# Reordering the start of a fused attention and feed-forward kernel: batch 0's front, and where batch 3 is loaded, cast and reduced

## The chip, the cores and the metric

The kernel runs on one core of one Trainium2 chip. The metric is device time in microseconds (us) for one execution, lower is better. Before the change the median of four runs is 284.23 us (284.03 to 284.37).

A core has five engines, each with its own instruction queue, worked in order: TensorE (PE; its weight loads are listed as PEld), VectorE (DVE), ScalarE (ACT), GpSimd (POOL) and SyncE (SP), which here only issues DMAs. Engines wait for each other by semaphores.

## The reference

q, k and v have shape (8 batches, 8 heads, 576 rows, 64 columns). The attention is the linear kind: softmax of q over its columns, softmax of k over its rows, a 64x64 product per head, and q times that product. Its result x (4608 x 512) goes through a two-layer feed-forward block with an exact GELU.

```python
q_s = np.exp(q - np.max(q, axis=-1, keepdims=True));  q_s /= np.sum(q_s, axis=-1, keepdims=True) + 1e-09
k_s = np.exp(k - np.max(k, axis=2, keepdims=True));   k_s /= np.sum(k_s, axis=2, keepdims=True) + 1e-09
kv  = np.einsum('bhsd,bhse->bhde', k_s, v)
x   = np.einsum('bhsd,bhde->bhse', q_s, kv)          # then (B*S, H*D)
h   = x @ w_in                                       # 512 -> 2048
out = (0.5 * h * (1.0 + erf(h / sqrt(2)))) @ w_out   # 2048 -> 512
```

## The kernel before, in words

The order of instructions is written out by hand (`tc.manual_schedule()`): each engine does its work in the order in which the program lists it, and a helper called early in the listing stands early in every queue that it uses, SP's among them.

The program works by chunks. Chunks 0 to 7 are batches 0 to 7, with the first 512 of the 576 rows each; chunk 8 holds the last 64 rows of all batches. For each batch there is a front and two phases.

The front of batch b:

- `load(b)`: three DMAs from SP, q, k and v, into buffers that exist twice (`f32in`, `bufs=2`), so that batch b + 2 reuses those of batch b. Batches 0 and 1 are loaded in parts.
- `exp_q`, `exp_k`: exponentials on ACT. `table(...)` is a tiny activation that makes ACT load the table of a function ahead of its use.
- `norm_q`: the row sums of exp(q) and their reciprocals on DVE, then the multiplication, on POOL unless DVE is named. `norm_q(b, 0, 2)` and `norm_q(b, 1, 2, nc.vector)` do the two halves of the heads, the first on POOL and the second on DVE.
- The transposed q (`qT`): for batches 0 and 1 by TensorE (`tp_mm`: eight transposes per half; `tp_evac`: the copy from PSUM, DVE by default; `tp_step` is both), later by a transposing DMA on SP (`xbar_step`).
- `cast_v`: v to bf16, one of four head pairs at a time, on DVE unless another engine is named; `cast_v_all` is all four on DVE.
- `kv_mm`: the product of exp(k) and v for two head pairs, 36 small matmuls; a column of ones in v gives the softmax sums of k along with it. `kv_norm` divides by them on DVE. `kv_step` is both halves and one division. The buffers for exp(k) and for v exist twice, by b modulo 2.
- `x_mm`, `x_evac`: q times kv, and its copy to SBUF as `xT` on DVE, or on ACT with "s". `x_all` is the whole.

Then `h_phase(c)`: 64 matmuls of `xT` with w_in, 16 tiles of four, and a GELU on ACT for each tile. `y_phase(c)`: four output tiles j of 16 matmuls each, accumulated in one of two PSUM buffers (`psum_y`, `bufs=2`); `y_out` copies each on DVE into one of four buffers and stores it from SP. Because DVE works in order, j = 2 can start only when DVE has reached and done the copy of j = 0. Chunk 0's y phase is written out separately and interleaved with batch 1's front (lines 464 to 511).

Both phases take a dictionary of insertions. In `h_phase` the key is the tile after whose GELU the insertion is listed; in `y_phase` it is (j, t), after matmul t of tile j. The front of a later batch is put into the phases of an earlier chunk in this way:

- lines 425 to 454, batch 0's front. `warm(n)` issues n matmuls on zeros into a scratch buffer.
- lines 464 to 511, chunk 0's y phase and batch 1's front.
- line 512, chunk 1's h phase with `cast_v_all(2)`; line 513, `load(3)`.
- lines 516 to 527, the exponentials of batches 2 and 3, and chunk 1's y phase with the rest of batch 2's front.
- lines 531 to 536, `front3`: the rest of batch 3's front, and `load(4)`; it is listed after the first GELU of chunk 2's h phase.
- lines 538 to 564: chunks 2 to 8, each with the front of the batch two further on.

At the beginning SP is given the loads of batch 0, of both weight matrices, and of batches 1 and 2, one after the other (lines 413 to 422). `cast_wi` and `cast_wo` convert the weights, the first two tiles of w_in on POOL.

Of the kernel before, what the change touches and what calls it, by code (L numbers as in the profile page):

```python
# [10 lines left out]
AF = mybir.ActivationFunctionType  # L11
# [5 lines left out]
def kernel(  # L17
# [16 lines left out]
    nc = tc.nc  # L34
# [6 lines left out]
    HP = H // 2  # L41
# [30 lines left out]
    def setup_tiles():  # L72
        nc.vector.memset(scr, 0.0)  # L73
        for i in range(2):
            nc.vector.memset(v_aug[i][:, :, :, D:D + 1], 1.0)

    def table(func):
        nc.scalar.activation(out=scr[:, 1:2], in_=scr[:, 0:1], func=func)  # L78
# [3 lines left out]
    def load_main(b, name, t, parts=1):  # L82
        f = f32in.tile([128, 2048], FP32, tag=name + "f")
        f = f.rearrange("p (h f) -> p h f", h=H)
        st[b][name + "f"] = f
        src = t[b, :, 0:M, :].rearrange("h (p j) d -> p h (j d)", j=J)
        n = H // parts
        for i in range(parts):
            nc.sync.dma_start(out=f[:, i * n:(i + 1) * n, :], in_=src[:, i * n:(i + 1) * n, :])
# [9 lines left out]
    def load(b):  # L99
        load_main(b, "q", q)  # L100
        load_pair(b, "k", k)
        load_pair(b, "v", v)
# [11 lines left out]
    def exp_q(b, parts=1):  # L114

        e = attn_sb.tile([128, J, H, D], BF16, tag="eq")
        st[b]["eq"] = e
        dst = e.rearrange("p j h d -> p h j d")
        src = st[b]["qf"]
        if b == B:  # L120
            src = src.rearrange("p j h d -> p h j d")
        else:
            src = src.rearrange("p h (j d) -> p h j d", j=J)
        if parts == 1:
            sets = [(slice(i, None, 4), slice(u, None, 4)) for i, u in ((0, 0), (1, 1), (2, 3), (3, 2))]
        else:
            sets = []
            for h in (0, 4):
                sets += [(slice(h + i, h + i + n), slice(h + u, h + u + n))
                         for i, u, n in ((0, 0, 2), (2, 3, 1), (3, 2, 1))]  # L130
        for i, u in sets:
            nc.scalar.activation(out=dst[:, i], in_=src[:, u], func=AF.Exp)  # L132

    def exp_k(b, parts=1):
        n = HP // parts
        for i in range(0, HP, n):
            nc.scalar.activation(  # L137
                out=ek[b % 2][:, i:i + n],
                in_=st[b]["kf"][:, i:i + n].rearrange("p x (n d) -> p x n d", n=NS),
                func=AF.Exp,  # L140
            )

    def cast_v(b, hp, eng=nc.vector):
        eng.tensor_copy(  # L144
            out=v_aug[b % 2][:, hp, :, 0:D],
            in_=st[b]["vf"][:, hp, :].rearrange("p (n d) -> p n d", n=NS),
        )

    def cast_v_all(b):
        for hp in range(HP):  # L150
            cast_v(b, hp)
# [18 lines left out]
    def kv_norm(b, h0, h1):  # L170

        ps = st[b]["kv"]
        m = h1 - h0
        rec = small.tile([128, 2, 2], FP32, tag="reck")
        nc.vector.reciprocal(rec[:, :, 0:m], ps[:, :, h0:h1, D])
        nc.vector.tensor_tensor(  # L176
            out=kvc[b].rearrange("p (h i) d -> p i h d", i=2)[:, :, h0:h1],
            in0=ps[:, :, h0:h1, 0:D],
            in1=rec[:, :, 0:m].unsqueeze(3).to_broadcast([128, 2, m, D]), op=ALU.mult,
        )  # L180

    def kv_step(b):
        kv_mm(b, 0)
        kv_mm(b, 1)
        kv_norm(b, 0, 2)
# [16 lines left out]
    def tp_mm(b, half):  # L202
        if half == 0:
            st[b]["qT"] = attn_sb.tile([128, J, HP, 128], BF16, tag="qT", name="qT")
        pool, tag = (psum_h, "h") if half == 1 else (psum_a, "a")
        ps = pool.tile([128, J, 2, 128], BF16, tag=tag)
        st[b][f"tp{half}"] = ps
        for i in range(2):
            hp = 2 * half + i
            for j in range(J):  # L210
                nc.tensor.transpose(  # L211
                    ps[:, j, i, :],
                    st[b]["eq"][:, j, 2 * hp:2 * hp + 2, :].rearrange("p h d -> p (h d)"),
                    identity,
                )

    def tp_evac(b, half, eng="v"):
        o = st[b]["qT"][:, :, 2 * half:2 * half + 2, :]
        if eng == "v":
            nc.vector.tensor_copy(out=o, in_=st[b][f"tp{half}"])  # L220
        else:
            nc.scalar.copy(out=o, in_=st[b][f"tp{half}"])

    def tp_step(b, half):
        tp_mm(b, half)
        tp_evac(b, half)
# [8 lines left out]
    def x_tile(b, hp, pool, tag):  # L235
        if "xT" not in st[b]:
            st[b]["xT"] = attn_sb.tile([128, HP, M], BF16, tag="xT", name="xT")
        st[b][f"x{hp}"] = pool.tile([128, M], FP32, tag=tag, name="ps")

    def x_mm(b, half):  # L240

        for bb in range(B if b == B else 1):
            for r in range(2):
                for i in range(2):
                    hp = 2 * half + i
                    pr = slice(r * 64, r * 64 + 64)
                    c = slice((r ^ i) * 64, (r ^ i) * 64 + 64)
                    ps = st[b][f"x{hp}"]
                    if b < B:
                        nc.tensor.matmul(  # L250
                            ps[c, :], kvc[b][pr, hp, :], st[b]["qT"][pr, :, hp, :],
                            start=True, stop=True,
                        )
                    else:
                        nc.tensor.matmul(
                            ps[c, bb * R:(bb + 1) * R], kvc[bb][pr, hp, :],
                            st[b]["qT"][pr, bb // 2, hp, bb % 2 * R:(bb % 2 + 1) * R],
                            start=True, stop=True,
                        )

    def x_all(b):

        for hp in range(HP):
            pool, tag = (psum_h, "h") if hp < 3 else (psum_a, "a")
            x_tile(b, hp, pool, tag)
        x_mm(b, 0)
        x_mm(b, 1)
        for hp, eng in ((0, "s"), (2, "v"), (1, "s"), (3, "v")):
            x_evac(b, hp, eng)
# [131 lines left out]
    def warm(n):  # L401
        ps = psum_y.tile([128, DM], FP32, tag="y")
        for i in range(n):
            nc.tensor.matmul(ps, zeros[:, 0:128], zeros, start=True, stop=True)  # L404
# [17 lines left out]
    load(2)  # L422
    nc.vector.memset(zeros, 0.0)
    setup_tiles()
    warm(30)


    table(AF.Exp)
    exp_q(0, parts=2)
    exp_k(0, parts=2)  # L430
    table(AF.Gelu)
    norm_q(0, 0, 2)
    norm_q(0, 1, 2, nc.vector)
    tp_step(0, 0)
    warm(5)
    cast_v(0, 0)
    cast_v(0, 1, nc.gpsimd)
    cast_v(0, 2, nc.gpsimd)
    cast_wi(0, wi[0], "p")
    cast_wi(1, wi[1], "p")  # L440
    tp_step(0, 1)
    for hp, pool, tag in ((0, psum_y, "y"), (1, psum_y, "y"), (2, psum_a, "a"), (3, psum_h, "h")):
        x_tile(0, hp, pool, tag)
    kv_mm(0, 0)
    kv_norm(0, 0, 1)
    x_mm(0, 0)
    x_evac(0, 0, "s")
    x_evac(0, 1, "s")
    cast_v(0, 3)
    kv_mm(0, 1)  # L450
    kv_norm(0, 1, 2)
    x_mm(0, 1)
# [26 lines left out]
    tp_step(1, 0)  # L479
    tp_step(1, 1)  # L480
    cast_v(1, 3)
    for t in (12, 13):
        for j in range(J):
            y_mm(0, yps[j], j, t)

    def y_end(j):
# [23 lines left out]
    y_out(0, yps[2], 2)  # L510
    y_out(0, yps[3], 3)
    h_phase(1, {12: [lambda: cast_v_all(2)]}, groups={0: 2})
    load(3)


    exp_q(2, parts=2)
    exp_k(2)
    exp_q(3)
    exp_k(3)
    table(AF.Gelu)  # L520
    y_phase(1, {
        (0, 15): [lambda: norm_q(2, 0, 2)],
        (1, 1): [lambda: norm_q(2, 1, 2, nc.vector)],
        (1, 12): [lambda: kv_step(2)],
        (1, 15): [lambda: xbar_step(2)],
        (3, 5): [lambda: x_all(2)],
    })


# [1 line left out]
    def front3():  # L531
        norm_q(3, 0, 2)
        norm_q(3, 1, 2, nc.vector)
        cast_v_all(3)
        xbar_step(3)
        load(4)

    for c in range(2, B + 1):
        nb = c + 2
        ins = {}  # L540
        if c == 2:
            ins[0] = [front3]
            ins[12] = [lambda: kv_step(3)]
        elif nb < B:
            ins[0] = [lambda nb=nb: load(nb)]
        elif nb == B:
            ins[0] = [load_qrest]
        h_phase(c, ins, groups={0: 2} if c == 2 else {})
        yi = {}
        if nb <= B:  # L550
            exp_q(nb)
            if nb < B:
                exp_k(nb)
            table(AF.Gelu)
            yi[(1, 0)] = [lambda nb=nb: norm_q(nb)]
            if nb < B:
                yi[(0, 8)] = [lambda nb=nb: cast_v_all(nb)]
            yi[(3, 0)] = [lambda nb=nb: xbar_step(nb)]
        if c < B:
            w = [lambda c=c: x_all(c + 1)]  # L560
            if nb < B:
                w.append(lambda nb=nb: kv_step(nb))
            yi[(2, 12)] = w
        y_phase(c, yi)
# [30 lines left out]
```

## Time and profile before

| what | value |
|---|---|
| median of four runs | 284.23 us |
| the profiled execution | 284.37 us |
| its span, first to last instruction | 282.6 us |
| TensorE busy | 274.0 us (97%) |
| ScalarE busy | 155.8 us (55%) |
| VectorE busy | 102.2 us (36%) |
| GpSimd busy | 32.2 us (11%) |
| moved by DMA | 50.10 MB, 177 GB/s over the span |
| end of the last warm-up matmul before the first transposes | 10.77 us |
| start of chunk 0's h phase | 16.00 us |
| start of chunk 1's h phase | 46.27 us |
| end of chunk 1's y phase | 75.95 us |

How to read the lines of a profile: times are in us from the span's start. A line of a timeline has the start, the duration, the engine (PEld is TensorE's weight load, SPq an issue on SP), the line of the kernel, the operation, the tile written and the tiles read, and the count of merged instructions; in brackets is how long the engine had been idle, and what ended the wait. A line of the chain of waits has a start, a duration, and what the end of the program hung on at that time. Matmuls are pipelined, so that their times overlap a little, and a small overlap is shown for other engines too.

### The profile page before, as it was taken

To read this page: it belongs to the slowest core of one execution; us is meant where nothing else is said; L and a number is where in the kernel's file an instruction comes from. 1 tells how busy PE (TensorE), PEld (TensorE's weight loads), DVE (VectorE), ACT (ScalarE), POOL (GpSimd) and SP (SyncE) were. 2 spreads that over 40 slices of the span, in tenths; PEclk is the share of its full clock that TensorE was granted. 3 is DMA by queue.
4 is the path that set the end of the run, shared out by engine and by line. 5 is a ranking of instruction groups with operands and counts; after the bars stand their busy time and mean duration, and the time that the engine had idled before them with its cause. 6 is when DMAs were issued, how large, how long until landed. Compare 5 with 4: busy or idle time off the path is not lost.

```text
span 282.6 us, 4588 instructions
## 1 busy us (share of the span) xinstructions
PE 274.0 (97%) x1939; PEld 126.5 (45%) x1939; DVE 102.2 (36%) x151; ACT 155.8 (55%) x241; POOL 32.2 (11%) x24
## 2 busy tenths in 40 slices
PE   8889999999999799999999999999999999999995
PEld 2444454444444344444444444444444444444443
DVE  2866586308580380065105520463005300130012
ACT  5566854689476814694368526862683364036400
POOL 0430050002020050005000500050004000000000
PEclk9999999999999999999999999999999999999999
DMA  6999999972459429911891279225601500120033
GB/s 241 399 389 430 396 403 407 321 288 72 128 68 351 168 75 195 399 59 57 197 374 61 77 181 352 98 77 155 145 0 74 148 2 0 74 77 0 2 74 75
DMA packets 44852, 50.10 MB, mean 177 GB/s; under 512 B 20384, under 2 KB 29856, under 8 KB 44576
## 3 DMA queue, kind: packets, MB, share of 16 engines
q1 hardware_dynamic: 44544, 49.68, 53.2%
q8 instruction: 15, 0.25, 0.4%
q10 hardware_dynamic: 288, 0.13, 0.2%
q14 instruction: 5, 0.04, 0.1%
HBM read 36.70 MB, written 9.44 MB: 163 GB/s over the span
## 4 chain that ended last, share of the span: by engine, by line
PE 87%; DVE 4%; DMA 4%; ACT 2%; SPq 1%; issue 1%; DVEq 0%; ACTq 0%
PE ps L294 39%; PE ps L304 39%; PE ps L404 4%; DMA f<-in_v_dram 4%; PE kv L165 2%; PE ps L250 1%; PE ps L326 1%; DVE v_aug L144 1%; DVE qsum L195 1%; SPq L97 1%; ACT ek L137 1%; ACT e L132 1%; PE ps L211 1%; DVE e L197 1%; SPq L230 0%
## 5 line engine op out<-in xcount | busy, mean ns | idle before, releaser
L304 PE MATMUL ps<-wo_bf,g 128*128 128x512 bf16 x560 | 124.4, 379 | 2.1 <-DVE y_sb L311 2.1
L294 PE MATMUL ps<-xT,wi_bf 128*128 128x512 bf16 x576 | 126.1, 379 | 0.0
L299 ACT ACTIVATE g<-ps 128x512 bf16<-128x512 f32 x144 | 85.6, 597 | 67.5 <-PE ps L294 67.5
L294 PEld LDWEIGHTS <-wi_bf 128*128 128x128 bf16 x576 | 56.1, 98 | 68.0 <-issue 0.5
L304 PEld LDWEIGHTS <-g 128*128 128x128 bf16 x560 | 53.9, 98 | 66.9 <-issue 3.2
L311 DVE COPY y_sb<-ps 128x512 f32<-128x512 f32 x35 | 23.9, 684 | 77.6 <-PE ps L304 77.3
L197 POOL TENSOR_TENSOR e<-e,recq 128x2048 bf16<-128x2048 bf16 (+1 forms) x9 | 25.7, 2854 | 180.3 <-DVE recq L196 158.3
L144 DVE CAST v_aug<-f 128x576 bf16<-128x576 f32 x27 | 18.6, 744 | 50.6 <-DMA f<-in_v_dram 50.6
L276 ACT CAST xT<-ps 128x512 bf16<-128x512 f32 x19 | 10.2, 588 | 35.3 <-PE ps L250 25.8
L195 DVE TENSOR_REDUCE qsum<-e 128x16 f32<-128x1024 bf16 (+1 forms) x13 | 21.0, 1619 | 15.3 <-ACT e L132 15.3
L132 ACT ACTIVATE e<-f 128x512 bf16<-128x512 f32 (+1 forms) x42 | 20.5, 556 | 1.4 <-DMA f<-in_q_dram 1.2
L137 ACT ACTIVATE ek<-f 128x2304 bf16<-128x2304 f32 (+1 forms) x10 | 17.3, 1729 | 1.6 <-DMA f<-in_k_dram 1.6
L274 DVE CAST xT<-ps 128x512 bf16<-128x512 f32 x15 | 9.7, 687 | 15.6 <-PE ps L250 12.8
L78 ACT ACT_TABLE_LOAD x9 | 11.5, 1283 | 2.8 <-issue 2.6
L404 PE MATMUL ps<-zeros 128*128 128x512 bf16 x35 | 10.8, 480 | 1.2 <-DVE scr L73 1.2
L132 ACT ACT_TABLE_LOAD x7 | 9.0, 1283 | 0.1
L165 PEld LDWEIGHTS <-ek 64*64 64x64 bf16 x576 | 6.3, 106 | 3.0 <-issue 1.4
L165 PE MATMUL kv<-v_aug,ek 64*64 64x65 bf16 x576 | 6.9, 193 | 0.3 <-DVE v_aug L144 0.2
L404 PEld LDWEIGHTS <-zeros 128*128 128x128 bf16 x35 | 4.0, 119 | 7.0 <-issue 3.9
L378 DVE CAST wi_bf<-w 128x512 bf16<-128x512 f32 (+1 forms) x8 | 6.6, 852 | 1.4 <-DMA w<-in_moe_w_in_dram 1.0
L397 DVE CAST wo_bf<-w 128x2048 bf16<-128x2048 f32 (+1 forms) x5 | 5.1, 1011 | 4.1 <-DMA w<-in_moe_w_out_dram 4.1
L250 PE MATMUL ps<-qT,kvc 64*64 64x512 bf16 x60 | 5.0, 390 | 1.4 <-DVE kvc L176 1.4
(28 smaller groups left out, 42.7 us busy)
## 6 DMA issues: line engine op xcount, KB each, us to landing
out_dram<-y_sb SPq DMA_DIRECT2D x32, 256.0 KB, 2.3
f<-in_k_dram SPq DMA_DIRECT2D x6, 1152.0 KB, 10.0
f<-in_v_dram SPq DMA_DIRECT2D x6, 1152.0 KB, 11.7
f<-in_q_dram SPq DMA_DIRECT2D x6, 1024.0 KB, 7.8
w<-in_moe_w_in_dram SPq DMA_DIRECT2D x6, 512.0 KB, 8.3
f<-in_k_dram SPq DMA_DIRECT2D x4, 576.0 KB, 10.0
f<-in_v_dram SPq DMA_DIRECT2D x8, 288.0 KB, 7.8
f<-in_q_dram SPq DMA_DIRECT2D x4, 512.0 KB, 8.6
```

What stands on the lines that cost most here:

```text
L78: nc.scalar.activation(out=scr[:, 1:2], in_=scr[:, 0:1], func=func)
L132: nc.scalar.activation(out=dst[:, i], in_=src[:, u], func=AF.Exp)
L137: nc.scalar.activation(out=ek[b % 2][:, i:i + n], in_=st[b]["kf"][:, i:i + n].rearrange("p x (n d) -> p x n d", n=NS), func=AF.Exp,)
L144: eng.tensor_copy(out=v_aug[b % 2][:, hp, :, 0:D], in_=st[b]["vf"][:, hp, :].rearrange("p (n d) -> p n d", n=NS),)
L165: nc.tensor.matmul(ps[c, i, half, 0:D + 1], ek[b % 2][pr, hp, n, :], v_aug[b % 2][pr, hp, n, 0:D + 1], start=(n == 0), stop=(n == NS - 1),)
L195: nc.vector.reduce_sum(out=qsum, in_=eq[:, :, hs, :], axis=AX.X)
L197: eng.tensor_tensor(out=eq[:, :, hs, :], in0=eq[:, :, hs, :], in1=recq.unsqueeze(3).to_broadcast([128, J, w, D]), op=ALU.mult,)
L294: nc.tensor.matmul(ps, wi_bf[:, dm, t * 128:(t + 1) * 128], xT[:, dm, :], start=(dm == 0), stop=(dm == NDM - 1),)
L299: nc.scalar.activation(out=g[:, t, :], in_=ps, func=AF.Gelu)
L304: nc.tensor.matmul(ps, st[c]["g"][:, t, j * 128:(j + 1) * 128], wo_bf[:, t, :], start=(t == 0), stop=(t == NDF - 1),)
L311: nc.vector.tensor_copy(out=y_sb, in_=ps)
L404: nc.tensor.matmul(ps, zeros[:, 0:128], zeros, start=True, stop=True)
```

## The change

In batch 0's front:

- 3 fewer warm-up matmuls at the start, and 2 instead of 5 after the first transposes;
- the first transposes are copied by ACT instead of DVE, and the loading of GELU's table comes after that copy;
- v's head pair 3 is cast on POOL with pairs 1 and 2, ahead of POOL's casts of w_in, instead of on DVE between the x products;
- the copy of the second transposes, still on DVE, stands behind the first division of kv instead of ahead of kv's matmuls.

For batch 3:

- `load(3)` is listed after batch 1's last cast of v, ahead of chunk 0's output stores, instead of after chunk 1's h phase;
- exp(k) of batch 3 comes ahead of its exp(q);
- `cast_v_all(3)` and `kv_step(3)` move from chunk 2's h phase into chunk 1's y phase, at (2, 2) and, behind `x_all(2)`, at (3, 5).

```diff
-    warm(30)
+    warm(27)
     table(AF.Exp)
     exp_q(0, parts=2)
     exp_k(0, parts=2)
-    table(AF.Gelu)
     norm_q(0, 0, 2)
     norm_q(0, 1, 2, nc.vector)
-    tp_step(0, 0)
-    warm(5)
+    tp_mm(0, 0)
+    tp_evac(0, 0, "s")
+    table(AF.Gelu)
+    warm(2)
     cast_v(0, 0)
-    cast_v(0, 1, nc.gpsimd)
-    cast_v(0, 2, nc.gpsimd)
+    for hp in range(1, HP):
+        cast_v(0, hp, nc.gpsimd)
     cast_wi(0, wi[0], "p")
     cast_wi(1, wi[1], "p")
-    tp_step(0, 1)
+    tp_mm(0, 1)
...
     kv_mm(0, 0)
     kv_norm(0, 0, 1)
+    tp_evac(0, 1)
     x_mm(0, 0)
     x_evac(0, 0, "s")
     x_evac(0, 1, "s")
-    cast_v(0, 3)
     kv_mm(0, 1)
...
     tp_step(1, 1)
     cast_v(1, 3)
+    load(3)
...
     h_phase(1, {12: [lambda: cast_v_all(2)]}, groups={0: 2})
-    load(3)
     exp_q(2, parts=2)
     exp_k(2)
+    exp_k(3)
     exp_q(3)
-    exp_k(3)
...
-        (3, 5): [lambda: x_all(2)],
+        (2, 2): [lambda: cast_v_all(3)],
+        (3, 5): [lambda: x_all(2), lambda: kv_step(3)],
...
     def front3():
         norm_q(3, 0, 2)
         norm_q(3, 1, 2, nc.vector)
-        cast_v_all(3)
         xbar_step(3)
         load(4)
...
             ins[0] = [front3]
-            ins[12] = [lambda: kv_step(3)]
```

## The prediction

> **What bounds the kernel now.** I read the busy shares first, then the chain that ended last, then the waits, then the order of time around the three places that the change touches.
>
> ```profile
> PE 274.0 (97%) x1939; PEld 126.5 (45%) x1939; DVE 102.2 (36%) x151; ACT 155.8 (55%) x241; POOL 32.2 (11%) x24
> DMA  6999999972459429911891279225601500120033
> PE ps L304 <- DVE y_sb L311: 2.1, 1, 2.1
> ```
>
> TensorE is busy for 97% of the span, so a change can pay only at TensorE's gaps or by removing its work. The second line (the DMA share in 40 slices of 7.07 us) shows transfers saturated from the second slice to the eighth: whatever waits there for a load cannot be hurried by computing faster. The third line is TensorE's longest wait on another engine, 2.1 us in one piece. The chain of waits, in order of time, says where it comes from:
>
> ```profile
> 75.95 0.69 DVE y_sb L311
> 76.64 1.14 DVE qsum L195
> ...
> 79.53 1.76 DVE e L197
> ...
> 85.73 10.41 DMA f<-in_v_dram
> 96.14 0.02 issue
> 96.16 2.73 DVE v_aug L144 x4
> 98.90 0.61 DVE y_sb L311
> 99.51 0.04 issue
> 99.55 2.96 PE ps L304 x13
> ```
>
> From 75.95 to 99.55 the end is set not by TensorE but by a relay: the last copy of y phase 1, batch 3's softmax of q on DVE, its transposing DMA and load(4) behind it on SP, the landing of batch 4's v, its four casts, and only then the copy that frees TensorE's buffer for j = 2 of y phase 2. The relay takes 99.55 - 75.95 = 23.60 us, counted from the end of y phase 1 ("y1 end" below). TensorE is busy for 21.50 us of that stretch and idle for 2.1. After 99.55 the chain is TensorE without a break.
>
> The front, in order of time:
>
> ```profile
> 10.60 0.61 PE L211 MATMUL ps<-identity,e 128*128 128x128 bf16 x8
> 11.05 1.24 PE L404 MATMUL ps<-zeros 128*128 128x512 bf16 x5
> 11.05 1.38 POOL L144 CAST v_aug<-f 128x576 bf16<-128x576 f32 x2 [1.79 <-DMA f<-in_v_dram]
> 12.67 0.48 PE L165 MATMUL kv<-v_aug,ek 64*64 64x65 bf16 x36
> 13.38 0.16 DVE L175 RECIPROCAL rec<-kv 128x2 f32<-128x2 f32 x1
> 16.00 0.39 PE L294 MATMUL ps<-xT,wi_bf 128*128 128x512 bf16 x1
> ```
>
> Real work waits behind warm-up matmuls: the casts of v parts 0 and 1 are nearly there when warm(5) runs, and kv(0) starts at 12.67. The second block of interest is batch 1:
>
> ```profile
> 42.03 0.74 DVE L144 CAST v_aug<-f 128x576 bf16<-128x576 f32 x1
> 43.44 0.17 DVE L175 RECIPROCAL rec<-kv 128x2 f32<-128x2 f32 x1 [0.66 <-PE kv L165]
> 44.28 0.41 PE L250 MATMUL ps<-qT,kvc 64*64 64x512 bf16 x4
> ```
>
> DVE casts the fourth part of v(1) just ahead of normalizing kv(1). That part's load was issued at 33.7 and took 8.2 us, so it lands at 41.9: there is little room to be earlier.
>
> **The front, part by part.** Warm-up: in the last stretch warm matmuls start every 0.216 us (in the first 5.95 us every 0.427), so 3 fewer end at 10.77 - 0.65 = 10.12. The first transposes' operand is ready (POOL's multiply, 7.36 + 1.90 = 9.26), so they run 10.12 to 10.6; warm(2) to 11.0; the second transposes (DVE's multiply ends at 10.34) to 11.5. The first cast of v on DVE no longer stands behind a copy: 10.36 to 11.1 (its load: issued 2.9, 7.5 us). POOL's cast of part 1 ends at 11.05 + 0.67 = 11.72, and this sets kv(0): 11.75 instead of 12.67.
>
> The copy of the first transposes goes to ACT, which is free at 10.77. No row has this shape on ACT. Bounds: 0.69 us (DVE's copy of the tile) to 1.16 us (ACT's 128x1152 exp); a line through ACT's 0.588 (512 columns) and 1.163 gives 1.05, which I take, as engine and width are nearest. It ends at 11.85. Gelu's table follows, 1.28 + 0.20, done at 13.35. The trace shows no copy under exp's table; should it force a reload, 1.28 more (both ends kept below). The Trainium skill ("ScalarE: Activation LUTs", "Table sets: the hidden batching unit") says that a plain copy is in every set, by which nothing would be added; no run here shows that.
>
> kv_norm(0) now precedes the second transposed copy on DVE. From a kv start to its x matmuls took 15.65 - 14.58 = 1.07 without that copy in the way, so the first x matmuls start at 12.82 (before 13.93), kv's second half at 13.25, and the second x matmuls at 14.32. The third extra cast on POOL ends before that: part 2 lands at 11.7, part 3 at 6.3 + 6.2 = 12.5, cast by 13.16; POOL is then free at 13.16, still ahead of w_in's first tile (13.88). h phase 0 thus starts at 14.32 + 0.41 = 14.73 instead of 16.07. ACT's first two x copies, 13.35 to 14.42, are in time; POOL's cast of w_in (13.88, four of 0.635) gives tiles 0 and 1 by 15.15, needed at 15.6, and tiles 2 and 3 by 16.42, needed at 16.46. The fourth w_in block (cast ends 22.19, needed 22.1) costs about 0.1. So y phase 0 starts 1.25 us earlier.
>
> Then batch 1's loads cap it. q(1)'s exp at 32.32 already waits for its load; it stays, and so do the multiplies up to 38.23, which are needed at 39.0. v(1)'s fourth part lands at 41.9, cast until 42.67; kv_norm stands behind it on DVE (0.17 + 0.29 with handovers 0.46), so x(1) starts at 43.15. Before: 44.28. Gain: the smaller of 1.25 and 1.13, **1.13 us** (0.87 with a reload in front).
>
> **load(3) earlier** adds nothing: the same three DMAs, now ahead of four y stores on SP. The engines are saturated until 61 either way. They wait on SP for the buffers of batch 1, last for the cast ending at 42.67, and the first store is ready only at 43.9. By the rate now seen (2.9 us for each of k and v), v(3) lands near 60 instead of 63.1, the stores near 62.5 instead of 53.8; y phase 1 reuses their buffers from 64. Cover 1.5 us or more. exp_k(3) before exp_q(3): both end at 71.0 as now.
>
> **cast_v_all(3)** moves on DVE from 81.20 to between y copies 1 and 2 of y phase 1, 4 casts, 2.73 us, 69.5 to 72.2. Behind it wait the copy of j = 2 (done at 72.9 instead of 72.5, whose buffer is wanted in y phase 2), and x(2)'s copies at 73.69. Nothing is late. In its old place it was beside the load, not in the relay: no gain either.
>
> **kv_step(3)** moves from h phase 2 (87.07) to y phase 1, behind x(2). 72 small matmuls, 0.64 (chain) to 0.78 us (group); I take 0.65. In the old place this work sat in front of the 2.1 us gap and cost nothing. In the new one it pushes y1 end, from which the relay of 23.60 us counts, so all of it is paid, and the gap becomes 2.10 + 0.65 = 2.75 us.
>
> **Sum**: -1.13 + 0.65 = -0.48 us. The profiled execution took 284.37 (span 282.6); the median is 284.23. From the median: **283.75**.
>
> The gap raises one more question. In the trace, 2.1 us of idleness left the clock warm: 13 matmuls from 99.55 take 2.96 us. The Trainium skill ("TensorE: Matmul & The Clock Gate", "Why this matters for your kernels") warns against idle gaps above some 3 us, after which the clock halves. By that rule 2.75 us stays just free of charge; no row here has such a gap.
>
> **Rivals.** (1) *The relay shortens, and kv(3) is free.* The transposing DMA of batch 3 took 5.4 us where the median of its kind is 3.8, and q, k, v queue behind it. If that eases by 0.65 or more, the gap does not grow: 284.23 - 1.13 = 283.1. Against it: nothing of what the change does stands beside that DMA.
> (2) *Slower: the loads take the whole front gain, and kv(3) is paid.* Place: the DVE queue at v(1)'s fourth cast. If that part lands at 43.0 instead of 41.9 (a load rate lower by 2.6%; stretches of the front move 373 to 408 GB/s), x(1) starts at 44.28 as now: 284.23 + 0.65 = 284.88. It decides from a surviving gain under 0.08 us. For it: DMA share above 1.0 throughout; against: nothing in the change adds bytes before that part.
> (3) *Slower: the widened gap drops the clock.* The 14 cold matmuls of the start cost 14 x (0.427 - 0.216) = 2.95 us: 286.7. For it: the gap does widen; against: 2.1 us did no harm.
> (4) *The front does only part*: ACT reloads a table, or its copy holds up x(0): gain 0.6 to 0.87, so 284.0 to 284.3.
>
> **How the numbers follow.** Forecast 0.55 (own range 283.4 to 284.1), rival 1 0.15, rival 2 0.17, rival 3 0.04, rival 4 0.09. A change of 0.2%, 0.57 us, is about what can be told from none: below 283.66 is faster, above 284.80 slower. The forecast lies 0.09 us from the first border, so I split it 0.25 faster, 0.30 same. Faster 0.25 + 0.15 = 0.40; same 0.30 + 0.09 = 0.39; slower 0.17 + 0.04 = 0.21. The range, 283.0 to 285.0, holds the forecast and rivals 1, 2 and 4 and leaves rival 3 out.
>
> **What will show it.** Right: h phase 0 starts near 14.7, x(1) near 43.2 with DVE's v cast in front of it; kv(3) in y phase 1; y1 end near 75.5; a TensorE wait of about 2.75 us on the y copy, and matmuls after it at full pace. Wrong: h phase 0 after 15.3, x(1) earlier than 43 or at 44, a wait of 2.1 or less, or slow matmuls behind it. I would be most wrong if v(4) came at a time not tied to y1 end.

## The result, and the profile after

| | executions | median | lowest to highest |
|---|---|---|---|
| before | 79 | 284.37 us | 282.81 to 287.17 |
| after | 53 | 283.29 us | 282.46 to 284.32 |

The ratio of the times is 0.9953, with a 95% interval of 0.9941 to 0.9965: faster by 0.5%. The profiled execution of after took 284.32 us (span 282.5), the longest of its kind, so what follows goes by its stretches and not by its total.

TensorE and its one long wait after the change (the busy shares, and the list of waits):

```profile
PE 273.8 (97%) x1933; PEld 126.4 (45%) x1933; DVE 102.1 (36%) x149; ACT 156.8 (55%) x242; POOL 32.8 (12%) x25
PE ps L304 <- DVE y_sb L311: 1.4, 1, 1.4
```

The gap ahead of j = 2 of y phase 2 shrank from 2.1 to 1.4 us, where the prediction had it grow to 2.75. The chain of waits, in order of time, from the last copy of y phase 1:

```profile
77.20 0.69 DVE y_sb L311
...
80.70 1.76 DVE e L197
...
84.66 0.71 SPq L97
...
85.42 10.42 DMA f<-in_v_dram
...
95.87 2.73 DVE v_aug L144 x4
98.60 0.61 DVE y_sb L311
...
99.25 2.97 PE ps L304 x13
```

The relay is still there, hop by hop, but it takes 99.25 - 77.20 = 22.05 us instead of 23.60. That is the gain. In these two traces nearly all of it lies ahead of v(4)'s transfer, which takes 10.41 and 10.42 us: from the end of batch 3's softmax to the start of that transfer it is 4.44 us before (81.29 to 85.73) and 2.96 after (82.46 to 85.42). There SP issues the transposing DMA and load(4); the transposing DMA took 5.4 us before and 3.7 after, and this is the issue of v(4) before:

```profile
83.56 2.13 SPq L97
```

y1 end itself came later, at 77.20 instead of 75.95. The front shows why (order of time, new front):

```profile
10.93 0.99 ACT L222 COPY qT<-ps 128x1024 bf16<-128x1024 bf16 x1
11.30 2.16 POOL L144 CAST v_aug<-f 128x576 bf16<-128x576 f32 x3 [1.98 <-DMA f<-in_v_dram]
12.02 0.47 PE L165 MATMUL kv<-v_aug,ek 64*64 64x65 bf16 x34 [0.41 <-POOL v_aug L144]
12.54 0.17 DVE L175 RECIPROCAL rec<-kv 128x2 f32<-128x2 f32 x1 [1.21 <-PE kv L165]
14.92 2.48 PE L294 MATMUL ps<-xT,wi_bf 128*128 128x512 bf16 x6
```

h phase 0 starts at 14.92 instead of 16.00, as forecast (14.73). But its first six matmuls take 2.48 us. The stretches of that time (TensorE's busy time, the granted clock, the DMA share, GB/s) tell the reason:

```profile
12.00:14.00 2.00, 1.37 (x74) 1.00 1.09 386
14.00:16.00 2.00, 1.42 (x8) 0.81 1.07 399
16.00:18.00 2.00, 2.00 (x6) 0.50 1.05 401
18.00:20.00 2.00, 2.00 (x9) 0.84 1.05 404
```

By these rows the clock was granted at half from 15.2 to 18.6. It had been full before: TensorE was busy for about 70% of 12 to 16 us, with waits of 0.4 to 0.6 us between small pieces of work. So this execution lost in h phase 0 (15.61 us instead of 13.92) more than the front had won. Most executions of after did not: of 54, 43 had a mean clock of 0.997 or more, with a median of 283.11 us, and 11 had 0.991 to 0.992, with 283.96. The front before is not free of it: the trace of batch 3 alone, which has that front, shows 0.50 from 16 to 18 us.

Of the kernel before, 93 executions beside the experiments have a mean clock on record: 49 at full clock (median 283.92 us), 22 at 0.993 to 0.994 (285.38), 14 at 0.987 to 0.988 (286.88), and 8 at 0.991 to 0.992 (284.06). A stretch of 3.4 us at half clock in a span of 282 lowers the mean by 3.4 x 0.5 / 282 = 0.006, so 0.994 fits one such stretch and 0.988 two. (The 0.992 of the execution above is its one stretch and a lower clock after the last matmul, 0.87 from 280 to 282 us, which delays nothing.) "Full clock" below means a mean of 0.996 or more.

### The profile page after: what moved, and what is told of

Same layout as the page of the kernel before. It is cut to its first block, busy times and chain, and to the rows that moved or that the text cites. A ratio compares the mean times of both kernels' runs of the same rounds, so it can differ in the third digit from the quotient of the medians.

```text
span 282.5 us, 4576 instructions
## 1 busy us (share of the span) xinstructions
PE 273.8 (97%) x1933; PEld 126.4 (45%) x1933; DVE 102.1 (36%) x149; ACT 156.8 (55%) x242; POOL 32.8 (12%) x25
## 4 chain that ended last, share of the span: by engine, by line
PE 84%; DMA 7%; DVE 3%; ACT 2%; SPq 1%; issue 1%; POOL 0%; ACTq 0%
PE ps L294 40%; PE ps L304 39%; DMA f<-in_v_dram 6%; PE kv L165 2%; PE ps L250 2%; DMA f<-in_q_dram 1%; PE ps L326 1%; DVE v_aug L144 1%; DVE qsum L195 1%; ACT ek L137 1%; ACT e L132 1%; DVE e L197 1%; SPq L230 0%; DVE y_sb L311 0%; ACT L132 0%
## 5 line engine op out<-in xcount | busy, mean ns | idle before, releaser
L294 PE MATMUL ps<-xT,wi_bf 128*128 128x512 bf16 x576 | 127.7, 383 | 0.0
L144 DVE CAST v_aug<-f 128x576 bf16<-128x576 f32 x26 | 17.9, 745 | 54.9 <-DMA f<-in_v_dram 54.9
L276 ACT CAST xT<-ps 128x512 bf16<-128x512 f32 x19 | 10.2, 588 | 32.0 <-PE ps L250 22.4
L404 PE MATMUL ps<-zeros 128*128 128x512 bf16 x29 | 8.5, 456 | 1.2 <-DVE scr L73 1.2
L378 DVE CAST wi_bf<-w 128x512 bf16<-128x512 f32 (+1 forms) x8 | 7.2, 913 | 2.7 <-DMA w<-in_moe_w_in_dram 2.5
L197 DVE TENSOR_TENSOR e<-e,recq 128x1024 bf16<-128x1024 bf16 x4 | 6.4, 1609 | 0.1
```

The lines of the kernel that those rows point to most:

```text
L144: eng.tensor_copy(out=v_aug[b % 2][:, hp, :, 0:D], in_=st[b]["vf"][:, hp, :].rearrange("p (n d) -> p n d", n=NS),)
L197: eng.tensor_tensor(out=eq[:, :, hs, :], in0=eq[:, :, hs, :], in1=recq.unsqueeze(3).to_broadcast([128, J, w, D]), op=ALU.mult,)
L294: nc.tensor.matmul(ps, wi_bf[:, dm, t * 128:(t + 1) * 128], xT[:, dm, :], start=(dm == 0), stop=(dm == NDM - 1),)
```

## The experiments

Each is timed beside the kernel before on the same chip. The runs came in three rounds on three chips, where the kernel before had full-clock medians of 283.94, 284.06 and 283.86 us; 283.92 is that of all its executions, and a difference between rows of different rounds is uncertain by some 0.2 us. Relay and load are each from one traced execution. "Relay" runs from the last copy of y phase 1 to the end of the copy that frees j = 2; "load" from the issue of batch 3's transposing DMA to the landing of v(4). With load(4) first v(4) no longer hangs on batch 3's softmax, and there is no relay.

| run | median | full clock: number, median | ratio to before, 95% interval | relay | load |
|---|---|---|---|---|---|
| before | 284.28 | 49 of 93, 283.92 | | 23.55 | 14.71 |
| after | 283.29 | 43 of 54, 283.11 | 0.9953 (0.9941 to 0.9965) | 22.00 | 13.24 |
| front alone | 284.27 | 9 of 12, 284.04 | 0.9972 (0.9944 to 1.0000) | 23.04 | 14.21 |
| batch 3 alone | 283.70 | 7 of 12, 283.13 | 0.9956 (0.9928 to 0.9983) | 21.70 | 12.95 |
| kv(3) put back | 283.70 | 8 of 12, 283.46 | 0.9968 (0.9937 to 0.9998) | 23.27 | 14.51 |
| load(4) first | 282.52 | 10 of 12, 282.38 | 0.9922 (0.9891 to 0.9953) | none | |
| refill moved in | 285.37 | 4 of 12, 284.27 | 1.0020 (0.9987 to 1.0054) | 22.81 | 14.05 |
| refill moved ahead | 284.39 | 6 of 12, 283.23 | 0.9989 (0.9953 to 1.0026) | 21.74 | 12.98 |
| load(4) first, gaps filled | 282.33 | 7 of 7, 282.33 | 0.9904 (0.9866 to 0.9941) | none | |
| load(3) late | 283.61 | 7 of 12, 283.28 | 0.9948 (0.9915 to 0.9981) | 21.88 | 13.12 |
| load(4) first, gaps filled, one memset | 281.56 | 6 of 6, 281.56 | 0.9899 (0.9860 to 0.9937) | none | |
| front alone, one memset | 283.32 | 10 of 12, 283.15 | 0.9961 (0.9932 to 0.9990) | 23.03 | 14.21 |
| after, one memset | 284.20 | 6 of 12, 283.49 | 0.9977 (0.9947 to 1.0006) | 21.82 | 13.07 |
| before, load(4) first | 281.83 | 9 of 11, 281.81 | 0.9913 (0.9880 to 0.9945) | none | |

**Front alone**: lines 425 to 454 as in after, the rest as before.

> Batch 0's front as changed, everything of batch 3 as before. Theory A (the forecast: the front is worth 1.13 us, held back by v(1)'s fourth part; the relay from y1 end is a fixed 23.6 us): 1.1 us below the kernel before, and the gap before j = 2 of y phase 2 stays near 2.1 us. Theory B (the front is worth little, since TensorE's sparse stretch sometimes drops its clock and the loads land when they land; the gain comes from a relay that lost 1.55 us because the casts of v(3) no longer run beside batch 3's transposing DMA): within 0.3 us of the kernel before, relay 23.6.

**Batch 3 alone**: the reverse.

> Batch 0's front as before, load(3), exp order, cast_v_all(3) and kv_step(3) as changed. Theory A: 0.65 us above the kernel before, gap 2.75 us, relay 23.6. Theory B: 0.65 - 1.55 = 0.9 us below it, gap about 1.2, relay about 22.05 and the transposing DMA of batch 3 at 3.7 us instead of 5.4.

**kv(3) put back** into chunk 2's h phase:

```diff
-        (3, 5): [lambda: x_all(2), lambda: kv_step(3)],
+        (3, 5): [lambda: x_all(2)],
...
             ins[0] = [front3]
+            ins[12] = [lambda: kv_step(3)]
```

> The changed kernel with kv_step(3) alone put back behind tile 12 of chunk 2's h phase. Theory A (kv in y phase 1 is paid in full): 0.65 us below the changed kernel, gap smaller by 0.65. Theory B (relay short enough to matter less): also up to 0.65 below, but no more than the gap that is left; relay 22.05 either way. If the move of kv was itself what shortened the relay: relay back to 23.6 and the time 0.9 above the changed kernel.

Measured: at full clock the front alone brings nothing (284.04 against 283.92) and batch 3 alone brings 0.79 us, the sign that theory A denies. Theory B had the side right and the cause wrong: with v's casts still early and only kv(3) put back, the load is slow again (14.51). So it is not the casts on DVE. In these five traces the relay is short where kv(3) is in y phase 1 and long where it is in h phase 2. Its time missed the 0.9 us that were expected above the changed kernel: it was 0.35 (283.46 against 283.11). The relay was longer by 1.27 us, but kv(3)'s 0.65 us no longer stood ahead of it.

What kv(3) does to a load can be read in the stretch of the load itself. First the kernel before, then kv(3) put back, then after; each has the GB/s in 40 slices from the transposing DMA's issue to v(4)'s landing, and, where there is one, the queue of instruction fetches:

```profile
GB/s 0 0 0 179 331 267 22 0 4 9 101 290 302 379 362 368 362 379 395 384 407 413 413 415 432 420 401 407 401 401 413 407 413 432 426 320 70 25 25 6
...
q8 instruction: 2, 0.03, 1.0%
```

```profile
GB/s 0 0 0 166 287 292 291 281 329 229 62 251 347 387 381 370 254 352 381 363 413 397 406 421 407 413 413 426 413 406 406 407 413 273 127 38 25 25 25 6
...
q8 instruction: 1, 0.02, 0.4%
```

```profile
GB/s 0 0 0 73 289 289 292 288 288 259 204 164 251 319 381 362 381 309 319 383 394 398 425 425 390 418 418 397 418 411 411 404 432 411 404 411 292 153 21 0
```

In the first two the load ends in a tail of three or four slices (0.36 us each) at 25 GB/s or less. 25 is one sixteenth of 400: by this rate fifteen of the 16 DMA engines are done and one is late, and v(4) has landed only when it is. A queue that carries instructions moved packets of 16 KB in that stretch, two before and one with kv(3) put back; in after it moved none, and the tail is gone. 16 KB at 25 GB/s are 0.65 us; the packets took 0.9 to 1.4. The first of the two before came at 83.2, inside the transposing DMA; the hole in slices 7 to 10 of that line follows it. That the packet made the hole is argued from this one trace.

In a whole execution this queue moves 15 such packets, and TensorE has 1939 matmuls and 1939 weight loads: one packet for some 260 instructions, if they are TensorE's. kv_step(3) has 72 matmuls and 72 weight loads. With them ahead of load(4), in y phase 1, the packet comes at 76.1 in after, before y1 end; with them inside h phase 2 it comes at 83.2 (before), 86.3 (kv(3) put back) and 87.1 (front alone), between the issue of the transposing DMA and the landing of v(4). That the packets are TensorE's refill was a guess until the next two runs.

**Refill moved in, refill moved ahead.** TensorE's instruction count is shifted by warm-up matmuls alone; the columns of zeros multiplied stay the same.

```diff
-    warm(27)
+    warm_narrow(48)      # 128 columns each; the second run: 100
+    warm(15)             # the second run: 2
```

> The changed kernel, whose 12 first warm-up matmuls of 512 columns are 48 of 128 columns: the same work on zeros, 72 more instructions for TensorE, so that its queue's refill by DMA (16 KB for 256 instructions) falls some 72 instructions earlier in the program: into load(4) instead of behind it. Theory B2 (kv_step(3)'s 144 instructions in chunk 2's h phase had put a refill into load(4), which made one of 16 DMA engines late and with it v(4); moving them took it out): the time from the transposing DMA's issue to the landing of v(4) goes from 13.0 to 13.3 back to 14.2 to 14.7 us, and the time is about 1 us above the changed kernel. Theory B1 (the casts or kv on the engines were in the DMA's way): 13.0 to 13.3 as in the changed kernel, same time.

> The same edit with 100 narrow matmuls for 25 wide ones, 150 more instructions: the refill should fall ahead of the transposing DMA. Theory B2: issue to landing of v(4) 13.0 to 13.3 us. Theory B1: the same. If the narrow matmuls themselves do harm, it shows here too. The front may be up to 1 us later, since narrow matmuls at full clock take longer for the same columns.

Measured: load 14.05 with the refill moved in, 12.98 with it moved ahead, and full-clock medians of 284.27 and 283.23. The load of the first, and then of the second, in the same view:

```profile
GB/s 0 0 0 135 291 291 291 275 316 296 175 204 367 387 353 373 344 349 382 406 413 413 420 413 413 400 400 406 460 393 387 393 400 367 171 79 26 26 20 0
...
q8 instruction: 1, 0.02, 0.4%
```

```profile
GB/s 0 0 0 54 289 289 290 290 287 310 199 139 303 338 347 372 388 353 325 373 379 417 419 405 419 419 405 419 398 412 419 405 412 419 412 419 355 163 78 0
```

The tail at 26 GB/s returns with the refill, though the program of that stretch is the same as in after. Theory B2 holds: a refill of TensorE's instruction queue inside load(4) makes v(4) about 1.1 us late. Where it falls matters too. In the ten traces with a relay, the load takes 14.05 to 14.71 us where a packet comes within 10.2 us of the transposing DMA's issue, and 12.95 to 13.24 where none does. Batch 3 alone belongs to the latter: it has a packet in the stretch, but 0.5 us ahead of the landing, and its load is the shortest (12.95).

The run with the refill moved in also shows what a gap can do to the clock. Its stretches around the gap (columns as above), and the piece of the order of time:

```profile
97.00:99.00 2.00, 0.49 (x3) 1.00 0.00 0
99.00:101.00 2.00, 1.33 (x4) 0.63 0.24 93
101.00:103.00 2.00, 2.00 (x7) 0.51 0.10 38
```

```profile
99.67 4.57 PE L304 MATMUL ps<-wo_bf,g 128*128 128x512 bf16 x13 [2.18 <-DVE y_sb L311]
```

In this execution the clock is halved for 3.4 us behind 2.18 us of idleness, and 13 matmuls take 4.57 us instead of 2.97: 1.6 us on top of the gap. Of that kernel's 12 executions 4 had a mean clock of 0.987.

**Load(4) first**, in after, and in the kernel before:

```diff
-        xbar_step(3)
         load(4)
+        xbar_step(3)
```

> The changed kernel with load(4) issued ahead of batch 3's transposing DMA, so that v(4) no longer hangs on batch 3's softmax. If the relay sets the end, as both theories say, the gap goes: 1.4 us (the gap of the changed kernel's profile) to 2.75 us (theory A) below the changed kernel. If TensorE were held by something else there: no change. Risk: the transposing DMA now lands behind 3.4 MB of loads, near 92 instead of 86.3; it is wanted at 102.

> The kernel before with load(4) ahead of batch 3's transposing DMA and nothing else. If the 2.1 us gap is what drops the clock in the kernel before's slower runs (mean clock 0.994 and 0.988): hardly such runs are left, apart from those of the front (0.991 to 0.992, some 0.994), and the time of full-clock runs is 2.1 us below the kernel before (284.0), near 281.9. If those clocks come from the front alone: their share stays near 4 in 10.

Measured: 0.73 us below after at full clock, less than the 1.4 that were expected at least (its last stores were longer, see "One memset"), and, in the kernel before, 2.11 us (281.81 against 283.92, expected 281.9). The transposed q lands near 92, as feared, and is not missed. In the latter's chain of waits, TensorE goes through j = 2 without a wait on another engine:

```profile
90.36 8.42 PE ps L304 x39
...
98.83 1.24 PE ps L304 x5
```

And of its 11 executions 2 had a lower clock (0.994), none 0.988, where the kernel before had 22 and 14 of 93. That fits a clock that drops behind the 2.1 us gap in some executions, but 11 are too few to show it: after with load(4) first has no such gap, and one of its 12 executions had 0.988 and took 285.02 us.

**Gaps filled**: five more matmuls on zeros between kv and x of batch 0, with load(4) first.

```diff
+    fill(1)
     kv_mm(0, 0)
+    fill(2)
...
     kv_mm(0, 1)
+    fill(2)
```

> The kernel with load(4) ahead of the transposing DMA, with five more matmuls on zeros in the gaps of batch 0's front (one ahead of kv's first half, two behind each half). If TensorE's sparse front is what drops its clock in some runs: hardly a run with a mean clock under 0.997, the median of the others as without them (282.4), and the mean 0.3 us lower. If the gaps are not the cause: the same share of such runs, time equal or 0.2 higher.

Measured: no execution of 7 below full clock, and none of 6 in the variant below; in the other seven kernels with the new front and unchanged warm-up it was 33 of 126. Some of the 33 may have dropped behind the gap ahead of j = 2; the one kernel that differs by the five matmuls alone had 2 of 12. So the filled gaps are a likely cure and not a proven one. The full-clock median did not move (282.33 against 282.38).

**Load(3) late**, behind chunk 1's h phase again:

> The changed kernel with load(3) back behind chunk 1's h phase. Both theories: v(3) lands near 63 instead of 60, well before its cast near 70, so the time is that of the changed kernel within 0.3 us. If the early load matters: slower.

Measured: 283.28 at full clock against 283.11 of after, which the spread of the executions covers. Nothing hangs on that move.

**One memset.** Why had the front alone brought nothing, when j = 2 started 0.9 us earlier in its trace (98.66)? The last stores took longer. From the rows of the output tile, the landing of the last stores, first the front alone, then after:

```profile
DMA to landing us min/median/max: 2.1/2.8/3.2
```

```profile
DMA to landing us min/median/max: 2.0/2.1/2.4
```

During them a second instruction queue moved one packet of 8 KB in the front alone and in two kernels with load(4) first, that in after's order and the one with filled gaps; not so in after. These three have 194 rows of VectorE in the trace; after and kv put back have 193, batch 3 alone 195, before 196. So one more row should move the packet:

```diff
         nc.vector.memset(scr, 0.0)
+        nc.vector.memset(scr, 0.0)
```

> Only batch 0's front changed, plus the same memset. Theory T: the front alone is worth what its relay starts earlier, 0.4 to 0.9 us, and only the meeting at the end hid it; with the memset 283.1 to 283.6 in runs of full clock, 1.0 below the front alone (284.04). Otherwise (the front is worth nothing): 284.0.

> The changed kernel plus the same memset: from 193 VectorE rows to 194. Theory T: now its last store is hit, 3.1 us instead of 2.1, and the time is up to 1.0 above the changed kernel (283.1 in runs of full clock), 284.1. Otherwise 283.1.

> The kernel with load(4) first and the front's gaps filled, plus one 0.06 us memset on VectorE at the start, which shifts VectorE's instruction count by one. Theory T (an 8 KB instruction refill meets the last output stores in programs with 194 VectorE rows and not in those with 193, 195 or 196; there the last store takes 3.1 us instead of 2.1): the last store takes 2.1 us and the time is 1.0 us below the same kernel without the memset (282.3), so 281.4. Otherwise the same 282.3.

Measured: the front alone 0.89 us faster (283.15 against 284.04), the filled kernel 0.77 us faster, and after slower, by 0.38 us at full clock (up to 1.0 was expected), with last stores of up to 3.1 us in its trace. So 0.06 us of work at the start can be worth 0.8 us at the end. The packet does not vanish, it moves. In the four traces where the last store takes 3.1 or 3.2 us, it comes 2.2 us after the first of the last four stores is issued. In the five where it comes 0.5 to 0.9 us after that, the last store takes 2.4 us, or 2.7 in the front alone with the memset:

```profile
DMA to landing us min/median/max: 2.3/2.5/2.7
```

In the other five, after among them, it comes when the stores have landed. The filled kernel with the memset, 281.56 us, 1.0% below before, is the fastest of the study; swapping two lines of the kernel before alone gives 281.83.

## Why the prediction was right, and where it was wrong

The side and the range were right, and 283.75 was 0.46 above the median. That it came so near was in part luck: its sum, -1.13 + 0.65, had one term right, one too large, and one missing, and the last two errors offset each other. The forecast's own range (283.4 to 284.1) does not hold 283.29, and a wait of 1.4 us is one of the signs that the prediction itself had named for being wrong ("a wait of 2.1 or less").

- *kv(3) is paid in full*: right. From h phase 1's start to y1 end before took 75.95 - 46.27 = 29.68 us and after 77.20 - 46.88 = 30.32: 0.64 (forecast 0.65). What it brought in the relay was more.
- *The relay is a fixed 23.60 us*: wrong, and this is the step that failed. Rival 1 ("the relay shortens") came true with 22.05, for a reason that the prediction had denied ("nothing of what the change does stands beside that DMA"). It had the right place, the transposing DMA's 5.4 us, and not what was in it. 144 TensorE instructions left that stretch, and the refill came 7 us earlier (76.1 instead of 83.2), ahead of the relay. I had costed a moved step by its time on its engine and by its DMAs, not by its instructions.
- *The front is worth 1.13 us*: the mechanism was right, the size was not. h phase 0 starts at 14.78 to 15.15 in the traces with the new front and the wide warm-up (forecast 14.73), and x(1) does hang on v(1)'s fourth part, through the cast ahead of kv_norm. The front alone, in order of time:

```profile
42.69 0.75 DVE L144 CAST v_aug<-f 128x576 bf16<-128x576 f32 x1 [0.94 <-DMA f<-in_v_dram]
43.36 0.16 DVE L175 RECIPROCAL rec<-kv 128x2 f32<-128x2 f32 x1
...
43.90 0.41 PE L250 MATMUL ps<-qT,kvc 64*64 64x512 bf16 x4 [0.42 <-DVE kvc L176]
```

  From landing to x(1) it is 1.23 us, as worked out (1.25). But I took 41.9 as the landing from one execution, and it was an early one: in the 13 later traces it lies between 41.88 and 42.94, in 12 of them later than 41.90. So the gain at x(1) is 0.4 us here, and between 0.0 and 0.8 in the traces of the new front without a half clock there, not 1.13. Rival 2's mechanism, a late landing, took that part.
- *2.1 us of idleness left the clock warm*: true of the one profiled execution. In the run with the refill moved in, 2.18 us did not; rival 3 had the right price in kind (a half clock) and too high in size: 1.6 us for one stretch and not 2.95, since it lasts 3.4 us. The Trainium skill ("TensorE: Matmul & The Clock Gate", "What's actually happening") gives the window as some 3.4 us and the cold clock as half, and the traces agree with both (15.2 to 18.6 us at 0.50). Its warning against gaps above about 3 us ("Why this matters for your kernels") is too mild here, where 2.18 us sufficed.
- *A copy under exp's table needs no reload*: right. The copy took 0.99 us (forecast 1.05) with no table load ahead of it, and the next one, at 11.94, is GELU's own. This agrees with the Trainium skill ("ScalarE: Activation LUTs", "Table sets: the hidden batching unit"), by which a plain copy is in every set.
- *load(3), the order of exp, and v(3)'s casts cost and bring nothing*: right for load(3), by the run with it late; the order of exp and the casts were not run alone, but with the casts early and kv(3) put back the relay stayed long (23.27). v(3) landed at 59.8 (forecast 60), the last store of chunk 0 at 62.4 (62.5).

The parts do not add up: 0.77 us for the front (with its memset) and 0.79 for batch 3, but 0.81 together, at full clock. A late v(1) can eat the front's share in any of them, and half of the front's gain may be its own refill, which fell once into load(4) instead of twice; which part is lost in the sum was not measured.

## What to carry to other kernels

A moved step takes its instructions along: where a load's landing sets the end, ask which refill of an instruction queue falls into it. Look for the relay first: here the cure was not to shorten the wait's legs but to issue the load ahead of the step that it never depended on, two lines that are worth more than the whole change (2.11 us against 0.81, at full clock). And a time read from one execution, a landing above all, is one draw: the landing that the forecast leaned on to within 1 us came later in 12 of 13 further traces.

## What was not expected of the hardware

- One 16 KB packet of TensorE's instruction fetch makes a 3.4 MB load land about 1.1 us later (12.98 to 14.05 us), by making, as the 26 GB/s of the tail say, one of 16 DMA engines late. In the last 0.5 us of the load it does no harm (12.95 us).
- One 8 KB packet of another queue, 2.2 us after the last stores are issued, goes with a last store of 3.1 to 3.2 us instead of 2.4 to 2.7 (four traces against ten). Whose queue it is, is argued from row counts and from three runs with one memset, not seen.
- In some executions the clock drops to half for 3.4 us: in one behind an idle gap of 2.18 us, in one in a front that keeps TensorE busy for 70% of the time with no gap above 0.6 us. With such gaps filled by five dummy matmuls it stayed full in 13 of 13 executions, against 10 of 12 without them.
